# Windowed attention and a feed-forward layer: q, k, v loads, weight conversion, exponent product and order of products rewritten

## The chip, the core and the metric

The kernel runs on one core of a Trainium2 chip. A core has five engines that run their own instruction streams: TensorE (PE in the profile, its weight loads PEld), VectorE (DVE), ScalarE (ACT), GpSimd (POOL) and SyncE (SP), which here issues loads and stores. The metric is the time of one execution on the device in microseconds, the median of several runs. Before the change it is 1030.34 us.

## The reference

Eight batches of 576 positions, eight heads of 64. Attention looks back over a window of 128 positions with a linear bias per head; its output, 4608 rows of 512, goes through two matrix products with a squared, clipped activation between them.

```python
scores = scale * np.matmul(q, k.transpose(0, 1, 3, 2))
bias = slopes[:, None, None] * (-np.abs(rel).astype(np.float32))[None, :, :]
mask = (rel >= 0) & (rel < window)                      # window = 128
scores = np.where(mask, scores + bias[None], -1000000000.0)
scores = scores - np.max(scores, axis=-1, keepdims=True)
attn = np.exp(scores)
attn = attn / (np.sum(attn, axis=-1, keepdims=True) + 1e-09)
x = np.matmul(attn, v)                                  # then transposed to 4608 x 512
...
h = x @ w_in                                            # 512 x 2048
g = np.where(pos, h, np.where(neg, 0.0, (h + beta) ** 2 / (4.0 * beta)))
return (g @ w_out).astype(np.float32)                   # 2048 x 512
```

q, k and v are float32. The two weight matrices arrive as float64.

## The kernel before

The 4608 rows are cut into twelve chunks of 384 rows (NCHUNK). For each chunk there is attention for four pairs of heads (pair p, chunk p // 4, so 48 pairs) and then sixteen blocks of 128 feed-forward columns (fc). While the feed-forward of chunk c runs, the attention of chunk c + 1 is computed between its products. `segments` is the list of attention steps and `ffn` the list of feed-forward steps; the last loop (L772 to L780) writes them down interleaved, in proportion, with the attention some steps ahead. The order in which each engine then runs its instructions is made from this by a planner that simulates the program with its own costs: an instruction written down earlier has precedence, but one that is ready may go ahead of one that is not. Within one engine the order so found is fixed in the program. `behind(instructions, f)` (L241) adds that what f writes down is issued after the named instructions, as far as it runs on the same engine as they do.

Most products are made of float16 halves: a float32 value becomes a high and a low float16, and a product becomes three (high by high, high by low, low by high). In chunks 0 and 1 attention itself is in float32; from chunk 2 on (LIGHT = 2) it uses halves as well. The halves need scales, powers of two from the largest exponent of what is to be split.

A feed-forward block is `layer1` (L582: twelve products of 384 columns on PE, L585 to L587; then u on ACT, L592, g on DVE, L593 and L594, its high half on ACT, L601, its low half on POOL, L602), and two blocks later `layer2` (L605: nine products of 512 columns, L616 to L618; in chunk 0 three float32 products, L613).

The turn of a pair p from pair 8 (p8) on, as L664 to L682 write it: row maxima of pair p + 4 (`reach_of`, L308: ACT over q and k, L318, DVE over v, L384), scores of blocks 0 and 1, scores of block 2 (`scores_of_pair`, L443, PE L453; each followed by DVE L476 and ACT L478 of the softmax), the split of v (L419), the values of pair p - 1 (`values_of_pair`, L544, PE L557, then ACT L566 and DVE L567, which make the x that layer1 reads), the transposes of head 2p (`weights_t`, L492: PE L497, ACT L509, DVE L510, POOL L512 and L514), the split of q and k of pair p + 1 (L360: ACT L367, DVE L368) with the load of pair p + 5 (`load_all`, L294: q L304, k L305, v L376, all issued by SP), and the transposes of head 2p + 1. The last pair of a chunk also makes the next chunk's scales: `level` (L320) and `scale_all` (L338).

q and k of a pair of chunk 3 or later are loaded into one of five tiles, chosen by p % 5 under the names of tiles that held weights before (L301). The three-row table `rels` of biases has the sixth of those places (L354). v has six buffers.

During chunk 0 the weights are converted. The float64 numbers are loaded as pairs of 32-bit words, low and high, w_in and w_out of a block into a tile each (`fetch_weights`, L184, issued by ACT). `float32_of` (L169) scales the high word as a float on ACT (L176), brings the low word's three top bits down on ACT (L177), shifts the high word by three on DVE (L178) and adds (L179). For a scale, the row maxima of a block are spread by POOL into a diagonal matrix (`spread`, L149, L152; L335 in `level`), which PE multiplies by ones in float32 (L157, L341), so that each partition holds all maxima; DVE takes the largest and keeps its exponent bits.

Of the kernel before, what the change touches and what calls it, by code (L numbers as in the profile page):

```python
# [8 lines left out]
F32 = mybir.dt.float32  # L9
# [11 lines left out]
def windowed_attention_then_ffn(  # L21
# [94 lines left out]

    sums = const.tile([P, 2, NQB, 2], F32, name="sums")
# [17 lines left out]
    ones = const.tile([P, P], F32, name="ones")  # L135
    G.memset(ones, 1.0)
# [12 lines left out]
    def spread(name, rows):  # L149

        diag[name] = ap1.tile([P, P], F32, name=f"d_{name}", tag="d", bufs=2)
        G.tensor_scalar(diag[name], ident, rows, None, ALU.mult)  # L152

    def scale_of(name, s, i):

        b = bank(f"m_{name}")[:, :P]
        T.matmul(b, ones, diag.pop(name), start=True, stop=True)  # L157
# [11 lines left out]
    def float32_of(w, name, out=None):  # L169

        low, high = w[..., 0], w[..., 1]
        f = stg.tile([P] + list(w.shape[1:-1]), F32, name=f"f_{name}", tag="stg")
        fi = f.bitcast(I32)


        S.activation(high.bitcast(F32), high.bitcast(F32), AF.Prelu, scale=2.0 ** -112, alpha=2.0 ** 32)  # L176
        S.activation(low, low.bitcast(U32), AF.Copy, scale=2.0 ** -29)  # L177
        V.tensor_scalar(fi, high, 3, None, ALU.logical_shift_left)  # L178
        V.tensor_tensor(fi if out is None else out.bitcast(I32), fi, low, ALU.add)  # L179
        return f  # L180

    raw = {}

    def fetch_weights(fc):  # L184
        w1 = rawp.tile([P, NCC, P, 2], I32, name=f"rawi{fc}", tag=f"rawi{fc % 3}")
        S.dma_start(w1, wi32[:, 2 * fc * P:2 * (fc + 1) * P].rearrange("(c p) (f w) -> p c f w", p=P, w=2))

        w2 = rawp.tile([P, DM, 2], I32, name=f"rawo{fc}", tag=f"rawo{fc % 3}")
        S.dma_start(w2, wo32[fc * P:(fc + 1) * P, :].rearrange("p (f w) -> p f w", w=2))
        raw[fc] = (w1, w2)  # L190
# [3 lines left out]
    def convert_in(fc):  # L194
        f = wide[fc] = wp.tile([P, NCC, P], F32, name=f"f_i{fc}", tag="f_i", bufs=3)
        float32_of(raw[fc][0], f"i{fc}", out=f)
        rows = column(f"rows_i{fc}", "rows")
        V.tensor_reduce(rows, f.rearrange("p c f -> p (c f)"), X, ALU.max, apply_absolute_value=True)
        spread(f"i{fc}", rows)
# [8 lines left out]
    def split_in(fc):  # L208
        if fc > 1:
            fall_in(fc)  # L210
        f, s1 = wide.pop(fc), s_in[:, fc:fc + 1]
        t = wi[fc] = wp.tile([P, 2, NCC, P], F16, name=f"wi{fc}", tag=f"wi{fc}")
        S.activation(t[:, 0], f, AF.Copy, scale=s1)
        V.scalar_tensor_tensor(t[:, 1], f, s1, t[:, 0], ALU.mult, ALU.subtract)  # L214
# [4 lines left out]
    def convert_out(fc):  # L219
        wf[fc] = wp.tile([P, DM], F32, name=f"wf{fc}", tag=f"wf{fc}")  # L220
        float32_of(raw[fc][1], f"o{fc}", out=wf[fc])
        S.activation(junk, wf[fc], AF.Abs, accum_out=rows_o[:, fc:fc + 1])
# [70 lines left out]

    def load_all(p):  # L294
# [3 lines left out]
        if c == LIGHT:  # L298
            t = wp.tile([P, 2 * CH + P], F32, name=f"qk_{p}", tag=f"wo{NPAIR + g}")
        else:  # L300
            tag = ("rawi0", "rawi1", "rawi2", "rawo0", "rawo1")[p % 5]  # L301
            t = rawp.tile([P, 2 * CH + P], F32, name=f"qk_{p}", tag=tag)
# [17 lines left out]
    def level(c):  # L320
# [12 lines left out]
        d = diag[c] = ap1.tile([P, 2, P], F32, name=f"d_{c}", tag="qr")  # L333
        for a in range(2):
            G.tensor_scalar(d[:, a], ident, top[:, a:a + 1], None, ALU.mult)  # L335
        tops[c, "i"] = iq

    def scale_all(c):  # L338

        b = bank(f"m_{c}")[:, :2 * P]  # L340
        T.matmul(b, ones, diag.pop(c).rearrange("p a w -> p (a w)"), start=True, stop=True)  # L341
# [11 lines left out]
        if "t" not in rels:  # L353
            rels["t"] = rawp.tile([P, NQB, 2 * P], F32, name="rels", tag="rawo2")  # L354
        rels[c] = rels["t"][:, c % 2], rels["t"][:, 2]
# [279 lines left out]
    for m in range(M1):  # L635
# [11 lines left out]
        if odd:  # L647
            part["v"] = [[lambda p=p: load_v(p + 4)]] if p < NPAIR else []
            part["v"] += [[lambda x=x: load_all(x)] for x in {5: (8, 9), 6: (10,), 7: (11,)}.get(p, ())]
# [14 lines left out]
    for p in range(M1 // 2, NP):  # L664
        c, g = divmod(p, NPAIR)
        new = p + NPAIR < NP
        if new:
            segments.append([lambda p=p: reach_of(p + NPAIR)])
        segments.append([lambda p=p: scores_of_pair(p, (0, 1))])
# [141 lines left out]
```

## Time and profile before

| | |
|---|---|
| median of 3 runs | 1030.34 us (1026.98 to 1031.44) |
| profiled execution, whole | 1030.51 us |
| its span, first to last instruction | 1028.3 us |
| PE busy | 975.1 us, 95% of the span |
| DVE busy | 742.2 us, 72% |
| ACT busy | 618.2 us, 60% |
| POOL busy | 374.7 us, 36% |
| mean granted TensorE clock | 0.979 |

Busy times of an engine are times in which an instruction of it is in work; PE's products overlap, so a full PE is not yet PE at its peak. Where an engine sat idle, a row shows in brackets how long and what ended it. "x12" counts instructions. "128x384" is partitions by elements. "granted clock" is the share of TensorE's clock that the chip let through. A row that ends "busy, mean ns | idle" gives the busy time of a group, the mean of one, and the idle time of the engine just before them.

### The profile page before, as it was taken

Reading aid. Unit: us, or ns where it says so; the run is one execution under the profiler, and the core shown is the slowest. Engines: PE = TensorE matmul, PEld = TensorE weight load, DVE = VectorE, ACT = ScalarE, POOL = GpSimd, SP = SyncE. Lnnn points to the kernel's source line nnn. Section 1 sums busy time; section 2 is a strip of 40 time slices with the busy share of each in tenths; the row PEclk is TensorE's granted clock in tenths of the full one; section 3 lists DMA queues with packets and bytes.
Section 4 is the critical chain, followed back from the end, with each engine's and each line's share of the span. In section 5 each row is a group of like instructions: output and inputs, shape, how many; then the busy total and the mean of one; then the engine's idle time right before and its main releaser. Section 6 shows DMA issues by size and latency. Waiting matters only on the chain.

```text
span 1028.3 us, 17951 instructions
## 1 busy us (share of the span) xinstructions
PE 975.1 (95%) x6218; PEld 548.8 (53%) x6218; DVE 742.2 (72%) x2128; ACT 618.2 (60%) x1547; POOL 374.7 (36%) x479
## 2 busy tenths in 40 slices
PE   7579999997899899899999999999999999999998
PEld 7446554554455455455555555555555555555554
DVE  5789889887767677777777777777777867775322
ACT  4678878665756655655755765765755755654332
POOL 5332211334344323433433433433434434334221
PEclk9889999999799999999999999999999999999999
DMA  8445442002101101201211201111101100000000
GB/s 258 159 154 168 160 142 85 1 11 73 52 22 57 57 24 35 69 30 39 68 40 40 74 24 47 57 30 57 60 29 57 50 2 1 32 1 1 32 1 31
DMA packets 53275, 59.88 MB, mean 58 GB/s; under 512 B 3520, under 2 KB 42432, under 8 KB 53184
## 3 DMA queue, kind: packets, MB, share of 16 engines
q1 hardware_dynamic: 42432, 41.96, 13.0%
q10 hardware_dynamic: 10752, 16.78, 4.8%
q8 instruction: 49, 0.80, 0.3%
q14 instruction: 42, 0.34, 0.1%
HBM read 49.28 MB, written 9.44 MB: 57 GB/s over the span
## 4 chain that ended last, share of the span: by engine, by line
PE 81%; DVE 8%; DMA 4%; ACT 3%; issue 2%; POOL 1%; ACTq 0%; SPq 0%; DVEq 0%; POOLq 0%
PE h L585 11%; PE h L587 11%; PE h L586 11%; PE acc L616 11%; PE acc L617 11%; PE acc L618 11%; PE s L453 5%; PE x L557 4%; PE p L497 3%; DMA vn<-in_v_dram 2%; PE acc L613 2%; PE x L536 1%; DVE g L593 1%; ACT z L478 1%; DVE g L594 1%
## 5 line engine op out<-in xcount | busy, mean ns | idle before, releaser
L602 POOL TENSOR_TENSOR gl<-g,gh 128x384 f16<-128x384 f32 x176 | 164.8, 936 | 394.1 <-ACT gh L601 375.9
L593 DVE SCALAR_TENSOR_TENSOR g<-u,half 128x384 f32<-128x384 f32 x176 | 121.0, 689 | 178.1 <-ACT u L592 167.9
L616 PE MATMUL acc<-wo,gh 128*128 128x512 f16 x528 | 200.0, 380 | 0.4 <-ACT wo L238 0.4
L617 PE MATMUL acc<-wo,gh 128*128 128x512 f16 x528 | 200.3, 379 | 0.0
L618 PE MATMUL acc<-wo,gl 128*128 128x512 f16 x528 | 197.0, 379 | 0.0
L601 ACT CAST gh<-g 128x384 f16<-128x384 f32 x176 | 89.7, 509 | 177.3 <-DVE g L594 124.7
L592 ACT ACTIVATE u<-h,shift,fall 128x384 f32<-128x384 f32 x176 | 116.4, 664 | 88.9 <-PE h L587 88.2
L478 ACT ACTIVATE z<-z,nmax 128x256 f32<-128x256 f32 (+2 forms) x288 | 137.7, 479 | 35.5 <-DVE nmax L476 34.8
L585 PE MATMUL h<-xh,wi 128*128 128x384 f16 x448 | 146.4, 328 | 3.7 <-DVE g L594 3.7
L587 PE MATMUL h<-xh,wi 128*128 128x384 f16 x448 | 147.4, 329 | 1.3 <-DVE wi L214 1.3
L586 PE MATMUL h<-xl,wi 128*128 128x384 f16 x448 | 147.2, 328 | 0.0
L476 DVE CUSTOM_DVE_ANT_0 z<-s,rels,z_of 128x256 f32<-128x256 f32 (+2 forms) x240 | 98.4, 459 | 26.8 <-PE s L453 26.4
L594 DVE SCALAR_TENSOR_TENSOR g<-h,gain,g 128x384 f32<-128x384 f32 x176 | 107.8, 614 | 3.8
L585 PE MATMUL h<-x,wi 128*128 128x384 f16 x320 | 105.3, 331 | 4.4 <-ACT x L566 3.1
L586 PEld LDWEIGHTS <-wi 128*128 128x128 f16 x768 | 75.7, 99 | 62.2 <-issue 9.2
L585 PEld LDWEIGHTS <-wi 128*128 128x128 f16 x768 | 75.5, 98 | 62.1 <-issue 6.6
L586 PE MATMUL h<-x,wi 128*128 128x384 f16 x320 | 105.9, 331 | 0.2 <-DVE x L567 0.2
L587 PE MATMUL h<-x,wi 128*128 128x384 f16 x320 | 105.9, 331 | 0.0
L587 PEld LDWEIGHTS <-wi 128*128 128x128 f16 x768 | 75.7, 99 | 54.6 <-issue 4.2
L512 POOL TENSOR_SCALAR_AFFINE_SELECT lu<-lu 128x768 f16<-128x768 f16 x80 | 72.5, 914 | 71.0 <-DVE lu L510 56.7
L618 PEld LDWEIGHTS <-gl 128*128 128x128 f16 x528 | 51.5, 98 | 58.6 <-issue 1.1
L616 PEld LDWEIGHTS <-gh 128*128 128x128 f16 x528 | 51.6, 98 | 52.0 <-issue 2.2
(154 smaller groups left out, 1555.4 us busy)
## 6 DMA issues: line engine op xcount, KB each, us to landing
out_dram<-o SPq DMA_DIRECT2D x36, 256.0 KB, 2.1
rawi<-in_moe_w_in_dram ACTq DMA_DIRECT2D x16, 512.0 KB, 3.7
rawo<-in_moe_w_out_dram ACTq DMA_DIRECT2D x16, 512.0 KB, 4.7
vn<-in_v_dram SPq DMA_DIRECT2D x32, 256.0 KB, 3.0
qk<-in_q_dram SPq DMA_DIRECT2D x40, 192.0 KB, 3.0
qk<-in_k_dram SPq DMA_DIRECT2D x28, 256.0 KB, 3.5
vn<-in_v_dram SPq DMA_DIRECT2D x16, 192.0 KB, 2.7
qk<-in_k_dram SPq DMA_DIRECT2D x12, 192.0 KB, 2.8
```

Source lines behind the costliest of these rows:

```text
L476: V.tensor_tensor_reduce(out=z[:, i, c0:], in0=pt[:, n, c0:], in1=r[:, c0:], op0=ALU.add, op1=ALU.min, scale=factor, scalar=3.0e38, accum_ ...
L478: S.activation(z[:, i, c0:], z[:, i, c0:], AF.Exp, bias=nmax[:, i:i + 1], scale=-1.0, accum_out=sm[:, i, 0:1])
L585: T.matmul(ph, wi[fc][:, 0, cc, :], xh, start=(cc == 0), stop=False)
L586: T.matmul(ph, wi[fc][:, 0, cc, :], xl, start=False, stop=False)
L587: T.matmul(ph, wi[fc][:, 1, cc, :], xh, start=False, stop=(cc == NCC - 1))
L592: first = S.activation(u, ph, AF.Relu, bias=shift[c] if c else quarter, scale=fall[c][:, col])
L593: V.scalar_tensor_tensor(g, u, half[c] if c else 0.5, u, ALU.min, ALU.mult)
L594: last = V.scalar_tensor_tensor(g, ph, gain[c][:, col] if c else fall[c][:, col], g, ALU.mult, ALU.max)
L602: G.tensor_tensor(gl, g, gh, ALU.subtract)
L616: T.matmul(a, gh[:, ts], wo[fc][:, 0], start=first, stop=False)
L617: T.matmul(a, gh[:, ts], wo[fc][:, 1], start=False, stop=False)
L618: T.matmul(a, gl[:, ts], wo[fc][:, 0], start=False, stop=last)
```

## The change

- `load_all`: from chunk 3 on, q and k go into three tiles of two halves each that are made once and kept; a half is chosen by the pair (p // 2 % 3 and p % 2). `rels` gets a lasting tile `near` of its own, with one row for the chunk's table instead of two.
- Order of a turn from pair 8 on: load of p + 5 first, row maxima of p + 4, then the values of p - 1 and the scores of blocks 0 and 1 in one step, scores of block 2, split of v, split of q and k of p + 1, then the transposes of both heads in one step. The mark after which the next chunk's feed-forward is written down moves with the values. The loads of chunks 1 and 2 get `behind` a head's transposes.
- Weights: w_in and w_out of a block come into one tile; the two ACT instructions each take both; a shift and an or in one DVE instruction join the words. The low word's factor becomes 0.9375 of what it was.
- Exponent product: no diagonal is built. The column of maxima, read as its upper 16 bits (a bfloat16), is broadcast as the weights of a bfloat16 product with a bfloat16 identity.

```diff
-    ones = const.tile([P, P], F32, name="ones")
-    G.memset(ones, 1.0)
+    ident16 = const.tile([P, P], BF16, name="ident16")
+    G.tensor_copy(ident16, ident)
...
     def spread(name, rows):
-        diag[name] = ap1.tile([P, P], F32, name=f"d_{name}", tag="d", bufs=2)
-        G.tensor_scalar(diag[name], ident, rows, None, ALU.mult)
+        diag[name] = rows
+    def across(b, rows):
+        r = rows.bitcast(BF16)
+        for a in range(rows.shape[1]):
+            T.matmul(b[:, a * P:(a + 1) * P], r[:, 2 * a + 1:2 * a + 2].broadcast_to([P, P]), ident16, start=True, stop=True)
...
-        T.matmul(b, ones, diag.pop(name), start=True, stop=True)
+        across(b, diag.pop(name))
...
+    def fetch_weights(fc):
+        w = raw[fc] = rawp.tile([P, 2, DM, 2], I32, name=f"raw{fc}", tag=f"raw{fc % 3}")
+        S.dma_start(w[:, 0].rearrange("p (c f) w -> p c f w", c=NCC),
+                    wi32[:, 2 * fc * P:2 * (fc + 1) * P].rearrange("(c p) (f w) -> p c f w", p=P, w=2))
+        S.dma_start(w[:, 1], wo32[fc * P:(fc + 1) * P, :].rearrange("p (f w) -> p f w", w=2))
+    def unfold(fc, which=slice(0, 2)):
+        low, high = raw[fc][:, which, :, 0], raw[fc][:, which, :, 1]
         S.activation(high.bitcast(F32), high.bitcast(F32), AF.Prelu, scale=2.0 ** -112, alpha=2.0 ** 32)
-        S.activation(low, low.bitcast(U32), AF.Copy, scale=2.0 ** -29)
-        V.tensor_scalar(fi, high, 3, None, ALU.logical_shift_left)
-        V.tensor_tensor(fi if out is None else out.bitcast(I32), fi, low, ALU.add)
+        S.activation(low, low.bitcast(U32), AF.Copy, scale=0.9375 * 2.0 ** -29)
+    def float32_of(fc, a, out):
+        V.scalar_tensor_tensor(out.bitcast(I32), raw[fc][:, a, :, 1], 3, raw[fc][:, a, :, 0], ALU.logical_shift_left, ALU.bitwise_or)
...
     def load_all(p):
-            tag = ("rawi0", "rawi1", "rawi2", "rawo0", "rawo1")[p % 5]
-            t = rawp.tile([P, 2 * CH + P], F32, name=f"qk_{p}", tag=tag)
+            i = p // 2 % 3
+            if i not in two:
+                two[i] = rawp.tile([P, 2, 2 * CH + P], F32, name=f"qk_{p}", tag=f"raw{i}")
+            t = two[i][:, p % 2]
...
-        if "t" not in rels:
-            rels["t"] = rawp.tile([P, NQB, 2 * P], F32, name="rels", tag="rawo2")
-        rels[c] = rels["t"][:, c % 2], rels["t"][:, 2]
+        rels[c] = near[:, 0], near[:, 1]
...
-            part["v"] = [[lambda p=p: load_v(p + 4)]] if p < NPAIR else []
-            part["v"] += [[lambda x=x: load_all(x)] for x in {5: (8, 9), 6: (10,), 7: (11,)}.get(p, ())]
+            part["v"] = [[lambda p=p: behind(done_t[2 * p], lambda: load_v(p + 4))]] if p < NPAIR else []
+            part["v"] += [[lambda p=p, x=x: behind(done_t[2 * p - 1], lambda: load_all(x))] for x in {5: (8, 9), 6: (10,), 7: (11,)}.get(p, ())]
...
-    for p in range(M1 // 2, NP):
+    for p in range(p8, NP):
         c, g = divmod(p, NPAIR)
         new = p + NPAIR < NP
-        if new:
+        if p + 5 < NP:
+            segments.append([lambda p=p: load_all(p + 5)])
+        if new and p > p8:
             segments.append([lambda p=p: reach_of(p + NPAIR)])
-        segments.append([lambda p=p: scores_of_pair(p, (0, 1))])
+        segments.append(([lambda p=p: values_of_pair(p - 1)] if p > p8 else []) + [lambda p=p: scores_of_pair(p, (0, 1))])
+        if p > p8 and g == 0:
+            ready.append(len(segments))
         if new and g == NPAIR - 1:
             segments.append([lambda c=c: level(c + 1)])
         segments.append([lambda p=p: scores_of_pair(p, (2,))])
         segments.append([lambda p=p: split_v(p)])
-        if p > M1 // 2:
-            segments.append([lambda p=p: values_of_pair(p - 1)])
-            if g == 0:
-                ready.append(len(segments))
+        if p == p8:
+            segments.append([lambda p=p: reach_of(p + NPAIR)])
         if new and g == NPAIR - 1:
             segments.append([lambda c=c: scale_all(c + 1)])
-        segments.append([lambda p=p: weights_t(2 * p)])
-        segments.append(([lambda p=p: split_qk(p + 1)] if p + 1 < NP else []) + ([lambda p=p: load_all(p + 5)] if p + 5 < NP else []))
-        segments.append([lambda p=p: weights_t(2 * p + 1)])
+        if p + 1 < NP:
+            segments.append([lambda p=p: split_qk(p + 1)])
+        segments.append([lambda p=p: weights_t(2 * p), lambda p=p: weights_t(2 * p + 1)])
```

More of the change, by code (lines that the diff above doesn't have):

```diff
@@ L115, in windowed_attention_then_ffn @@
                     compare_op=ALU.is_ge, fill=NEG)
+    near = const.tile([P, 2, 2 * P], F32, name="near")
     sums = const.tile([P, 2, NQB, 2], F32, name="sums")
@@ L167, in windowed_attention_then_ffn @@
     wo32 = w_out.bitcast(I32)
[L169 to L176, printed above, removed]
-        S.activation(low, low.bitcast(U32), AF.Copy, scale=2.0 ** -29)
-        V.tensor_scalar(fi, high, 3, None, ALU.logical_shift_left)
-        V.tensor_tensor(fi if out is None else out.bitcast(I32), fi, low, ALU.add)
-        return f
     raw = {}
     def fetch_weights(fc):
[L185 to L190, printed above, removed]
+        w = raw[fc] = rawp.tile([P, 2, DM, 2], I32, name=f"raw{fc}", tag=f"raw{fc % 3}")
[4 more added lines that the diff above has]
+        low, high = raw[fc][:, which, :, 0], raw[fc][:, which, :, 1]
+        S.activation(high.bitcast(F32), high.bitcast(F32), AF.Prelu, scale=2.0 ** -112, alpha=2.0 ** 32)
+        S.activation(low, low.bitcast(U32), AF.Copy, scale=0.9375 * 2.0 ** -29)
+    def float32_of(fc, a, out):
+        V.scalar_tensor_tensor(out.bitcast(I32), raw[fc][:, a, :, 1], 3, raw[fc][:, a, :, 0], ALU.logical_shift_left, ALU.bitwise_or)
     wide = {}
     def convert_in(fc):
-        f = wide[fc] = wp.tile([P, NCC, P], F32, name=f"f_i{fc}", tag="f_i", bufs=3)
-        float32_of(raw[fc][0], f"i{fc}", out=f)
+        f = wide[fc] = wp.tile([P, DM], F32, name=f"f_i{fc}", tag="f_i", bufs=3)
+        unfold(fc)
+        float32_of(fc, 0, f)
         rows = column(f"rows_i{fc}", "rows")
-        V.tensor_reduce(rows, f.rearrange("p c f -> p (c f)"), X, ALU.max, apply_absolute_value=True)
+        V.tensor_reduce(rows, f, X, ALU.max, apply_absolute_value=True)
         spread(f"i{fc}", rows)
@@ L211, in split_in @@
         f, s1 = wide.pop(fc), s_in[:, fc:fc + 1]
-        t = wi[fc] = wp.tile([P, 2, NCC, P], F16, name=f"wi{fc}", tag=f"wi{fc}")
+        t = wp.tile([P, 2, DM], F16, name=f"wi{fc}", tag=f"wi{fc}")
+        wi[fc] = t.rearrange("p s (c f) -> p s c f", c=NCC)
         S.activation(t[:, 0], f, AF.Copy, scale=s1)
@@ L220, in convert_out @@
         wf[fc] = wp.tile([P, DM], F32, name=f"wf{fc}", tag=f"wf{fc}")
-        float32_of(raw[fc][1], f"o{fc}", out=wf[fc])
+        float32_of(fc, 1, wf[fc])
         S.activation(junk, wf[fc], AF.Abs, accum_out=rows_o[:, fc:fc + 1])
@@ L292, in load_qk @@
             DMA.dma_start(kr[r, j, :n], k[g * P + j * D:g * P + (j + 1) * D, (c + 1) * CH - n:(c + 1) * CH])
+    two = {}
     def load_all(p):
@@ L332, in level @@
         V.tensor_reduce(top[:, 1:2], tops.pop(c)[:, :NPAIR], X, ALU.max)
-        d = diag[c] = ap1.tile([P, 2, P], F32, name=f"d_{c}", tag="qr")
-        for a in range(2):
-            G.tensor_scalar(d[:, a], ident, top[:, a:a + 1], None, ALU.mult)
+        diag[c] = top
         tops[c, "i"] = iq
@@ L340, in scale_all @@
         b = bank(f"m_{c}")[:, :2 * P]
-        T.matmul(b, ones, diag.pop(c).rearrange("p a w -> p (a w)"), start=True, stop=True)
+        across(b, diag.pop(c))
         i_2[c], s_2[c] = column(f"i_2{c}", "i_2", 3, 2), column(f"s_2{c}", "s_2", 3, 2)
```

## The prediction

> **What bounds the kernel now.** I read the page first, then the busy time by stretches cut at each chunk's first L594 (16 of that line in each stretch, one chunk of the feed-forward), then the timeline where a stretch is long.
>
> ```profile
> span 1028.3 us, 17951 instructions
> ...
> PE 975.1 (95%) x6218; PEld 548.8 (53%) x6218; DVE 742.2 (72%) x2128; ACT 618.2 (60%) x1547; POOL 374.7 (36%) x479
> ```
> ```profile
> 66.20:174.00 107.80, 100.71 (x447) 58.65 (x448) 97.22 (x305) 90.52 (x208) 23.86 (x36) 0.98 0.45 149
> 174.00:267.80 93.80, 82.14 (x543) 45.29 (x543) 77.33 (x208) 60.56 (x151) 32.80 (x34) 0.93 0.12 38
> 267.80:347.90 80.10, 77.16 (x506) 41.96 (x506) 58.15 (x169) 47.73 (x124) 31.48 (x38) 0.98 0.13 41
> 347.90:430.10 82.20, 78.15 (x530) 42.91 (x530) 58.10 (x169) 48.04 (x124) 31.56 (x40) 0.98 0.14 45
> ...
> 506.70:583.60 76.90, 76.90 (x514) 42.22 (x512) 58.02 (x166) 46.84 (x123) 30.28 (x38) 1.00 0.15 48
> 583.60:659.80 76.20, 76.20 (x531) 42.25 (x529) 58.19 (x166) 47.75 (x123) 30.93 (x40) 1.00 0.14 43
> ```
>
> The columns after the length are PE, PEld, DVE, ACT and POOL busy, then granted clock and DMA. From 430 us on a chunk takes 76.2 to 76.9 us and PE has no idle time: there only less PE work, or fewer changes between its shapes, can gain. Three chunks are longer than that mean of 76.55: by 17.25 (93.80), 3.55 (80.10) and 5.65 us (82.20), 26.45 together. The chunk in which the weights are converted takes 107.80 with DVE at 97.22, PE at 100.71 and ACT at 90.52: three engines near full, so neither alone is the limit. With the 26 us ahead of it:
>
> ```profile
> sum 134.00, PE 118.91 PEld 72.15 DVE 118.80 ACT 109.20 POOL 33.36; mean PE 19.82 PEld 12.03 DVE 19.80 ACT 18.20 POOL 5.56
> ```
>
> From 40 to 174 us PE is idle for 134.00 - 118.91 = 15.1 us.
>
> The 17.25 us lie at one place, on PE, then on the other engines:
>
> ```profile
> 248.87 1.15 PE L497 MATMUL p<-ident,ep 128*128 128x128 f32 x6
> 251.88 0.23 PE L453 MATMUL s<-h 64*128 64x128 f16 x2 [1.86 <-ACT h L367]
> ...
> 257.63 0.79 PE L453 MATMUL s<-h 64*128 64x256 f16 x5 [3.38 <-DVE nmax L476]
> 258.35 2.13 PE L557 MATMUL x<-lu,vs 128*64 128x256 f16 x24
> 263.55 0.80 PE L585 MATMUL h<-x,wi 128*128 128x384 f16 x2 [3.07 <-ACT x L566]
> ...
> 268.57 0.48 PE L585 MATMUL h<-x,wi 128*128 128x384 f16 x1 [1.34 <-DVE g L594]
> ```
> ```profile
> 254.38 1.06 POOL L514 TENSOR_SCALAR_AFFINE_SELECT lu<-lu 128x768 f16<-128x768 f16 x1
> ```
> ```profile
> 253.61 0.34 SPq L304 DMA_DIRECT2D qk<-in_q_dram  x1
> ```
> ```profile
> 256.79 0.52 ACT L318 ACTIVATE junk<-qk 128x384 bf16<-128x384 f32 x1 [4.46 <-DMA qk<-in_q_dram]
> ...
> 263.03 0.47 ACT L566 ACTIVATE x<-x 128x384 f16<-128x384 f32 x1
> ```
>
> The feed-forward of chunk 2 (L585) needs x of pair 11, the result of the values product L557. That product's weights were ready when POOL ended, 254.38 + 1.06 = 255.4, but it stood on PE behind the scores of pair 12 (251.88, 257.63) and ran at 258.35. Its copy L566 then stood on ACT behind softmax work that had been held 4.46 us by L318, a row maximum of q that waited for a load issued at 253.61 only. So two causes are in series: the order values after scores, and late loads.
>
> **The change part by part.**
>
> *Loads a turn ahead, six halves.* `load_all(p+5)` goes from the end of turn p to its start, and the slot it writes was last read by pair p-1 (six halves), not by p (five tags). Its three triggers cost SP 0.34 us each or a little more and SP is idle most of the time; behind them stand only later loads and the stores. The wait that this can shorten is
>
> ```profile
> ACT junk L318 <- DMA qk<-in_q_dram: 43.1, 23, 4.5
> ```
>
> 43.1 us of ACT's idle time; on PE it shows only where PE has nothing else queued, which is the 26.45 us above. But L318 runs as soon as the written-out order thinks its load has landed, and pair 18's load still follows the split of pair 12 in the same way; so I do not count the ACT wait as gone. The `behind` around the early loads ties instructions of one engine; the loads are issued by SP, the named instructions by ACT, DVE and POOL, so I cost it at nothing. Were it to hold the loads back, it could lose no more than the 15.1 us over again.
>
> *Values ahead of scores.* In the new order the values of p-1 come first, then the scores (0, 1) of p. At the place above the product could start at 255.4 instead of 258.35, its copy would be ahead of pair 12's softmax on ACT, and L585 could go on at about 255.4 + 1.2 (24 products at full clock) + 0.5 (L566) + 0.5 (DVE's low half, taken as long as ACT's) = 257.6 instead of 263.55: 5.9 us. With L585 running, the 1.34 us at 268.57 has cover, and of the 17 us at half clock around it (granted clock 0.93 over the stretch, 0.07 x 93.8 = 6.6 us of PE's time) I take 3. So 10 of the 17.25 us, bounds 0 and 17.25. The same two causes stand at 330 and 425 us; of 3.55 + 5.65 = 9.2 I take 4, bounds 0 and 9.2.
>
> *In the steady chunks* the groups of one turn are
>
> ```profile
> 599.07 0.82 PE L497 MATMUL p<-ident,ep 128*128 128x128 f32 x6
> ...
> 599.82 0.28 PE L453 MATMUL s<-h 64*128 64x256 f16 x1
> ...
> 604.52 0.82 PE L453 MATMUL s<-h 64*128 64x256 f16 x12
> ...
> 604.85 1.67 POOL L514 TENSOR_SCALAR_AFFINE_SELECT lu<-lu 128x768 f16<-128x768 f16 x2
> ...
> 609.92 0.42 PE L453 MATMUL s<-h 64*128 64x192 f16 x5
> ...
> 610.27 1.18 PE L557 MATMUL x<-lu,vs 128*64 128x256 f16 x24
> ```
>
> one score alone, eleven and one, then five and 24 values. After the change 24 values and twelve scores stand together and six scores by themselves: the number of groups between feed-forward products stays, except that the lone score may vanish or another appear. A lone one costs at most its 0.28 us; over 32 turns of eight chunks 9 us either way. I take 0.
>
> *Shift-or and joined tile.* Per block DVE now runs two pairs of
>
> ```profile
> L179 DVE CUSTOM_DVE_ANT_0 wf<-rawo,f_o 128x1024 uint16<-128x1024 uint16 x16 | 11.5, 720 | 0.0
> ...
> L593 DVE SCALAR_TENSOR_TENSOR g<-u 128x384 f32<-128x384 f32 x16 | 9.1, 572 | 3.1 <-ACT u L592 2.9
> ...
> L176 ACT ACTIVATE rawi<-rawi 128x512 f32<-128x512 f32 x16 | 10.8, 678 | 4.8 <-DMA kz<-in_k_dram 2.8 <-issue 1.2 <-ACT lu L501 0.6
> ...
> L178 DVE TENSOR_SCALAR f_i<-rawi 128x512 int32<-128x512 int32 x16 | 6.8, 423 | 0.3 <-ACT rawi L176 0.3
> ```
>
> L178 and L179, 0.42 + 0.72 = 1.14 us. One scalar_tensor_tensor of 512 elements takes their place. Its nearest row is L593 with constants, 0.572 us for 384; the step from 384 to 512 is
>
> ```profile
> L368 DVE SCALAR_TENSOR_TENSOR h<-qk,s_k,h 128x512 f16<-128x512 f32 x2 | 1.4, 738 | 0.0
> L368 DVE SCALAR_TENSOR_TENSOR h<-qk,s_q,h 128x384 f16<-128x384 f32 x2 | 1.2, 613 | 0.1
> ```
>
> 0.125 us, so 0.70 us: 0.44 less, 32 times, 14 us of DVE. ACT's four instructions of 0.67 become two of 1024 elements. The step by size on ACT:
>
> ```profile
> 24.48 0.39 ACT L478 ACTIVATE z<-z,nmax 128x128 f32<-128x128 f32 x1
> ...
> 24.86 0.49 ACT L478 ACTIVATE z<-z,nmax 128x256 f32<-128x256 f32 x1
> ```
>
> 0.10 per 128, so 0.67 + 0.40 = 1.07 each: 2.68 becomes 2.14, 16 x 0.54 = 8.6 us of ACT. Against it w_in's float32 waits for both, 2.14 instead of 1.34 us, and the first of them for the second landing too; the loads run two blocks (2 x 6.7 us) ahead, which covers that, and L592 can stand up to 0.4 us longer behind an ACT instruction.
>
> *Bfloat16 product of exponents.* The diagonal that POOL built goes; PE takes the column itself.
>
> ```profile
> PE m_i L157 <- POOL d_i L152: 6.8, 5, 3.2
> ...
> PE m_x L157 <- POOL d_x L152: 3.4, 2, 2.1
> ```
> ```profile
> L152 POOL TENSOR_SCALAR d_i<-ident,rows_i x16: 599/802/1965, 35.0 to 155.1; 128x128 f32<-128x128 f32 x16
> ```
>
> Seven waits of PE, 10.2 us; with 0.8 us less ahead of each, about 5.6 go. Together with DVE's 14 and ACT's 8.6 this acts on the 15.1 us that PE idles from 40 to 174; PE's own 118.9 us stay. I take half, 7 us; bounds 0 and 15.1. From chunk 2 on the two float32 products of a chunk go:
>
> ```profile
> 246.69 0.59 PE L341 MATMUL m<-d,ones 128*128 128x256 f32 x2
> 247.12 0.38 PE L618 MATMUL acc<-wo,gl 128*128 128x512 f16 x1
> ```
>
> 0.43 us from one start to the next. Two bfloat16 ones of 128 columns are not in the trace; below they cost nothing, above as much as two of the six float32 transposes at 599.07 (0.75 / 6 = 0.125 each). I take the upper one, 0.43 - 0.25 = 0.18, ten times: 2 us, bounds 2 and 4. The single `near` tile for the mask makes L356 wait for the last L476 of the chunk before, on the same engine and in that order already: nothing.
>
> **The sum.** 10 + 4 + 0 + 7 + 2 = 23 us less. The profiled execution took 1030.5 us (span 1028.3 and 2.2 around it), the median of the runs 1030.3, so no correction: 1007.5 us.
>
> [...]
>
> **Rivals.**
>
> *Half rate of shift-or.* If the two bitwise steps cost twice the streaming, 0.20 + 2 x 0.50 = 1.20 us against 1.14: DVE gains nothing and the half of 15.1 falls to the POOL part alone, about 2. Then 1030.5 - 18 = 1012.5. The float32 rows speak against it. Chance 0.05.
>
> *The loads and the order were not what held.* At 251.88 PE waited for the split of pair 12, whose scale needs all four pairs; at 248.87 for the softmax. If these follow the new order as they did the old one, and the conversion stretch is held by PE, only 2 or 3 us are left: 1028. For it speaks that L318 can again be issued before its load has landed; against it that L557 was ready 3 us before it ran. Chance 0.15.
>
> *A new wait: values for POOL (slower).* After the transposes at 599.07 the last POOL select ends at 604.85 + 1.67 = 606.5, but the scores went at 604.52 and the values only at 610.27, 3.8 us after POOL. If the values stand where the scores stood, PE waits up to 606.5 - 604.5 = 2.0 us in each of 40 turns. Above 23 / 40 = 0.6 us a turn the change loses. At 1 us: 1007.5 + 40 = 1047. Against it: the written order comes from a planner that knows POOL's work, and feed-forward products can stand in between. Chance 0.15.
>
> *All of it.* 17.25 + 9.2 + 15.1 + 4 = 45.5 us less, 985. Chance 0.15.
>
> **How the numbers follow.** My forecast has 0.50, with its own range of 995 to 1020. Less than 0.5%, about 5 us, cannot be told from no change: faster holds the forecast, the half rate and all of it, 0.70; same 0.15; slower 0.15. The range goes to 982 (all of it, and a few of the 9 us of lone scores) and to 1042 (most of the new wait).
>
> **What would show it.** Right: no PE idle time over 2 us between 245 and 270, clock 1.00 there, L557 ahead of the next pair's first L453; the three long chunks nearer to 76.5; the conversion chunk near 101, one DVE row near 0.70 us in place of two. Wrong: PE waiting at L557 for POOL turn after turn, the chunks from 430 us on longer than 77, or DVE's shift-or at 1.2 us. If the chunks from 430 on change by over 1 us each, my zero for the grouping was the mistake.

## The result and the profile after

The changed kernel takes 1142.44 us (median of 4 runs, the kernel before 1030.12 beside it): 1.108 times as long, 95% interval 1.104 to 1.113. The forecast was 1007.5 us, so even its sign was wrong. One of the four, the one first profiled, took 1364.22 us at a mean granted clock of 0.73, with 0.75 for up to 232 us on end; it is left out of the ratio, and the rows below are those of the next profiled run (1138.5 us, mean granted clock 0.939).

Span, busy time of the engines, and the granted clock in 40 slices, after:

```profile
span 1136.8 us, 17773 instructions
...
PE 1009.0 (89%) x6199; PEld 560.2 (49%) x6199; DVE 739.1 (65%) x2096; ACT 626.8 (55%) x1515; POOL 341.5 (30%) x440
...
PEclk9899999988998998997998999899799899799899
```

The span grew by 108.5 us. DVE, ACT and POOL have about as much work as before, or less. PE's busy time grew by 33.9 us with 19 instructions fewer, and its idle time from 53.2 to 127.8 us, by 74.6. So two thirds of the loss is idle time of PE. The other third is nearly the same products at a lower clock: the mean granted clock fell from 0.979 to 0.939, and the stretches at half clock grew from 46 to 142 us. The 24 products of the values took 2.13 us at a granted clock of 0.50 and 1.18 us at 1.00 (258.35 and 610.27 in the prediction); so half of PE's busy time in these stretches, an estimate of what the lower clock cost, is 12 us before and 45 after. From the tenth slice on the clock dips every three or four slices; a slice is 28.4 us, so that is about once a chunk.

The same stretches as in the prediction, cut at each chunk's first second half of g (now L598), after:

```profile
66.20:166.00 99.80, 93.40 (x417) 54.41 (x418) 90.71 (x282) 87.17 (x181) 10.71 (x18) 1.00 0.48 160
166.00:263.20 97.20, 83.32 (x548) 44.74 (x546) 75.59 (x208) 61.86 (x150) 29.88 (x32) 0.91 0.13 42
263.20:349.60 86.40, 78.33 (x506) 42.48 (x507) 56.80 (x165) 48.84 (x124) 28.80 (x34) 0.95 0.14 42
349.60:441.60 92.00, 81.21 (x530) 43.90 (x530) 59.98 (x169) 48.65 (x123) 30.45 (x38) 0.95 0.12 36
...
534.70:622.20 87.50, 80.12 (x506) 43.19 (x507) 56.04 (x164) 48.70 (x124) 28.88 (x34) 0.93 0.13 41
622.20:714.50 92.30, 81.41 (x530) 43.97 (x530) 60.99 (x168) 48.67 (x122) 30.21 (x38) 0.94 0.12 36
```

The conversion chunk is 8.0 us shorter (107.80 to 99.80). Every chunk behind it is longer, by 116.5 us together, and the steady ones now take 85 to 94 us: that is where the time went. Before they took 73.9 to 77.0; the 76.2 to 76.9 of the prediction are two of these seven chunks. Three waits on PE stand out; of them only the first is among the waits listed for the kernel before, with 5.0 us:

```profile
PE h L589 <- DVE g L598: 31.4, 8, 5.9
PE x L561 <- POOL lu L518: 30.5, 14, 6.3
PE p L501 <- DVE ep L493: 17.1, 5, 5.0
```

One turn of a steady chunk on PE (start, length, line, output<-inputs, shapes, count; the products of the feed-forward, L589 to L591 and L620 to L622, are left out):

```profile
559.97 0.82 PE L501 MATMUL p<-ident,ep 128*128 128x128 f32 x6
...
568.29 0.30 PE L561 MATMUL x<-lu,vs 128*64 128x256 f16 x1
568.52 0.28 PE L457 MATMUL s<-h 64*128 64x128 f16 x4
568.74 1.01 PE L561 MATMUL x<-lu,vs 128*64 128x256 f16 x17
569.68 0.56 PE L457 MATMUL s<-h 64*128 64x128 f16 x8
...
574.16 0.28 PE L457 MATMUL s<-h 64*128 64x256 f16 x1
575.13 0.50 PE L457 MATMUL s<-h 64*128 64x256 f16 x5
...
582.06 0.82 PE L501 MATMUL p<-ident,ep 128*128 128x128 f32 x6
...
591.03 0.30 PE L561 MATMUL x<-lu,vs 128*64 128x256 f16 x1
591.25 0.29 PE L457 MATMUL s<-h 64*128 64x128 f16 x4
```

And what the values (L561) of 591.03 stand for, on POOL:

```profile
584.26 0.86 POOL L516 TENSOR_SCALAR_AFFINE_SELECT lu<-lu 128x768 f16<-128x768 f16 x1 [2.35 <-DVE lu L514]
...
585.95 0.86 POOL L516 TENSOR_SCALAR_AFFINE_SELECT lu<-lu 128x768 f16<-128x768 f16 x1
586.77 1.99 POOL L518 TENSOR_SCALAR_AFFINE_SELECT lu<-lu 128x768 f16<-128x768 f16 x2
```

Read the turn as a chain. Transposes at 582.06; copies on ACT and DVE; POOL's four selects, done at 586.77 + 1.99 = 588.8; values at 591.03; and only among the values, from 591.3 on, the next pair's scores, whose softmax must pass before their transposes can come. In the rows of the kernel before that the prediction shows, the scores of the next pair (604.52) stood ahead of the values (610.27), so that POOL's work of one pair (604.85 to 606.5) and the softmax of the next ran at the same time. Its first DVE step, before:

```profile
605.38 0.48 DVE L476 CUSTOM_DVE_ANT_0 z<-s,rels,z_of 128x256 f32<-128x256 f32 x1 [0.55 <-PE s L453]
```

Now one pair's attention follows the other's end to end: 591.03 - 568.29 = 22.7 us. Four of them are 91 us, and the steady chunks take 85 to 94.

The same for 32 turns (pairs 12 to 43), worked out from the starts of these products on PE, means in us; the twelfth score is the last of blocks 0 and 1:

| kernel | 12th score to last transpose | last transpose to next pair's 12th score | last transpose to first values | turn |
|---|---|---|---|---|
| before | 13.60 | 5.79 | 11.06 | 19.38 |
| after | 14.67 | 7.92 | 6.26 | 22.59 |

3.21 us a turn, 32 times, is 103 of the 116.5 us. The values come 4.8 us earlier than before, as was meant; the scores, which start the next pair's chain, come 2.1 us later, and their way to the last transpose takes 1.1 us more.

While a turn lasts PE has feed-forward products to run. At a chunk's end they run out, because the next chunk's need the values of the last pair. PE there, after:

```profile
605.72 0.82 PE L501 MATMUL p<-ident,ep 128*128 128x128 f32 x6
...
610.45 0.27 PE L561 MATMUL x<-lu,vs 128*64 128x256 f16 x1 [0.30 <-POOL lu L518]
...
612.23 0.98 PE L561 MATMUL x<-lu,vs 128*64 128x256 f16 x17 [0.74 <-POOL lu L518]
...
614.64 0.24 PE L457 MATMUL s<-h 64*128 64x192 f16 x1 [1.43 <-DVE nmax L480]
...
622.91 0.48 PE L589 MATMUL h<-x,wi 128*128 128x384 f16 x1 [4.80 <-DVE g L598]
```

PE waits for the select, for the softmax, and then 4.80 us for the first g of the new chunk, with nothing else to run. Around this gap 0.50 of the clock was granted, from 614.8 to 628.4 us, and the steady chunks have a granted clock of 0.92 to 0.95 where they had 0.98 to 1.00.

What the change did to the conversion chunk can be read from the groups of 40 to 174 us before and 40 to 166 us after, on PE (busy us, mean ns | idle us ahead of the group, and what ended it). Before:

```profile
L157 PE MATMUL m_i<-d_i,ones 128*128 128x128 f32 x30 | 6.6, 300 | 7.0 <-POOL d_i L152 6.8
...
L157 PE MATMUL m_x<-d_x,ones 128*128 128x128 f32 x4 | 1.0, 326 | 3.4 <-POOL d_x L152 3.4
```

After:

```profile
L501 PE MATMUL p<-ident,ep 128*128 128x128 f32 x33 | 5.5, 276 | 4.3 <-ACT xh L582 2.4 <-DVE ep L493 1.9
...
L159 PE MATMUL m_i<-ident,rows_i 128*128 128x128 bf16 x15 | 3.3, 220 | 0.8 <-DVE rows_i L201 0.8
...
L159 PE MATMUL m_x<-ident,rows 128*128 128x128 bf16 x2 | 0.4, 219 | 0.0
```
```profile
40.00:166.00 126.00, 112.15 (x523) 68.78 (x523) 111.74 (x358) 107.92 (x232) 16.41 (x32) 0.99 0.50 162
```

The 10.2 us of waits for POOL's diagonal are gone, but PE still idles 126.00 - 112.15 = 13.9 us, against 15.1: other waits (4.3 us ahead of the transposes, 0.3 before) took their place. Of the 8.0 us, 6.8 came out of PE's busy time, 118.91 to 112.15. The m_i and m_x rows give 7.6 - 3.7 = 3.9 of that: the 15 and 2 float32 products ran as 30 and 4 instructions, the bfloat16 ones as 15 and 2. Much of the rest came with the clock: 0.97 was granted over 40 to 174 us before, with 0.83 from 60 to 80, and 0.99 over 40 to 166 after.

DVE and ACT in the conversion, groups by shape over the whole span, after:

```profile
L187 ACT ACTIVATE raw<-raw 128x1024 f32<-128x1024 f32 x16 | 18.4, 1151 | 4.8 <-DMA kz<-in_k_dram 3.7 <-ACT lu L505 0.6 <-issue 0.4
...
L192 DVE SCALAR_TENSOR_TENSOR wf<-raw 128x512 int32<-128x512 int32 x16 | 12.2, 762 | 0.0
...
L192 DVE SCALAR_TENSOR_TENSOR f_i<-raw 128x512 int32<-128x512 int32 x16 | 11.0, 688 | 1.0 <-ACT raw L188 0.7
```

### The profile page after: what moved, and what is told of

The parts are those of the page before. It is cut to its first block, busy times and chain, and to the rows that moved or that the text cites. A ratio compares the mean times of both kernels' runs of the same rounds, so it can differ in the third digit from the quotient of the medians.

```text
span 1362.5 us, 17773 instructions
## 1 busy us (share of the span) xinstructions
PE 1260.8 (93%) x6199; PEld 633.3 (46%) x6199; DVE 738.7 (54%) x2096; ACT 633.8 (47%) x1515; POOL 336.0 (25%) x440
## 4 chain that ended last, share of the span: by engine, by line
PE 84%; DVE 7%; DMA 4%; ACT 3%; issue 1%; POOL 1%; SPq 0%; ACTq 0%; DVEq 0%
PE h L589 12%; PE h L590 12%; PE h L591 12%; PE acc L620 11%; PE acc L621 11%; PE acc L622 11%; PE s L457 4%; PE acc L617 4%; PE x L561 3%; DMA vn<-in_v_dram 3%; PE p L501 3%; ACT z L482 1%; PE x L540 1%; DVE g L597 1%; DMA raw<-in_moe_w_out_dram 1%
## 5 line engine op out<-in xcount | busy, mean ns | idle before, releaser
L597 DVE SCALAR_TENSOR_TENSOR g<-u,half 128x384 f32<-128x384 f32 x176 | 113.0, 642 | 362.1 <-ACT u L596 336.1
L620 PE MATMUL acc<-wo,gh 128*128 128x512 f16 x528 | 244.3, 463 | 0.0
L621 PE MATMUL acc<-wo,gh 128*128 128x512 f16 x528 | 243.1, 460 | 0.0
L622 PE MATMUL acc<-wo,gl 128*128 128x512 f16 x528 | 237.5, 462 | 0.0
L589 PE MATMUL h<-xh,wi 128*128 128x384 f16 x448 | 176.4, 396 | 18.3 <-DVE g L598 17.1
L591 PE MATMUL h<-xh,wi 128*128 128x384 f16 x448 | 178.3, 398 | 0.0
L590 PE MATMUL h<-xl,wi 128*128 128x384 f16 x448 | 178.0, 397 | 0.3 <-DVE xl L583 0.2
L480 DVE CUSTOM_DVE_ANT_0 z<-s,near,z_of 128x256 f32<-128x256 f32 (+2 forms) x240 | 99.0, 460 | 87.2 <-PE s L457 87.1
L590 PEld LDWEIGHTS <-wi 128*128 128x128 f16 x768 | 87.7, 114 | 120.5 <-issue 68.5
L589 PE MATMUL h<-x,wi 128*128 128x384 f16 x320 | 126.7, 399 | 16.9 <-DVE g L598 15.2
L589 PEld LDWEIGHTS <-wi 128*128 128x128 f16 x768 | 87.3, 114 | 92.6 <-issue 40.3
L591 PE MATMUL h<-x,wi 128*128 128x384 f16 x320 | 128.4, 401 | 0.0
L590 PE MATMUL h<-x,wi 128*128 128x384 f16 x320 | 128.0, 400 | 0.2
L591 PEld LDWEIGHTS <-wi 128*128 128x128 f16 x768 | 88.7, 116 | 80.9 <-issue 13.5
L598 DVE SCALAR_TENSOR_TENSOR g<-h,gain,g 128x384 f32<-128x384 f32 x176 | 108.1, 615 | 3.9
L622 PEld LDWEIGHTS <-gl 128*128 128x128 f16 x528 | 58.4, 111 | 83.2 <-issue 75.6
L561 PE MATMUL x<-lu,vs 128*64 128x256 f16 (+1 forms) x888 | 70.6, 296 | 24.6 <-POOL lu L518 24.6
```

Source lines behind the costliest of these rows:

```text
L561: T.matmul(px[r, q0 * P:q1 * P], vs[:, a, i + b0, r], lus[j][:, b, first:first + q1 - q0, :].rearrange("p a w -> p (a w)"), start=(n == 0) ...
L589: T.matmul(ph, wi[fc][:, 0, cc, :], xh, start=(cc == 0), stop=False)
L590: T.matmul(ph, wi[fc][:, 0, cc, :], xl, start=False, stop=False)
L591: T.matmul(ph, wi[fc][:, 1, cc, :], xh, start=False, stop=(cc == NCC - 1))
L597: V.scalar_tensor_tensor(g, u, half[c] if c else 0.5, u, ALU.min, ALU.mult)
L598: last = V.scalar_tensor_tensor(g, ph, gain[c][:, col] if c else fall[c][:, col], g, ALU.mult, ALU.max)
```

## Experiments

The causes that were to be told apart: the order of values and scores; the new place of the loads; that values and scores stand in one step; the lead with which the attention is written down; POOL's selects; and the parts that have nothing to do with the order (halves, joined tile, shift-or, product). Each comparison is with the kernel before on the same chip, 1029.5 to 1031.0 us. Chunk lengths are cut as above.

**The changed kernel again.** No edit.

> The changed kernel once more, for a profile at full granted clock. Its earlier profile, at a granted clock of about 0.75, shows at each chunk boundary the first products of the next chunk (L589) held some 6 us for DVE's L598. Theory A (order): values of p-1 and scores of p in one step make the turn one serial chain (scores, softmax, transposes, POOL, values, next scores), so x of the last pair comes after the chunk's feed-forward products have run out; expects the idle time again at 9 or 10 boundaries, 5 to 8 us each, with half clock behind each, 1135 to 1145 us. Theory B (loads): DVE and ACT are held by row maxima of v, q, k whose loads come late; expects the same time, but DVE and ACT idle for DMA inside each boundary for most of the PE idle time.

1138.61 us, ratio 1.104 (1.096 to 1.112). The slowdown is there again; its trace is the one read above.

**The old turn.** The turn loop of the kernel before (values behind the split of v, transposes apart, loads after the split), all else changed; then the same with the load at the turn's start; then the changed loop with only the values and the ready mark moved back.

```diff
 # old turn
-        if p + 5 < NP:
-            segments.append([lambda p=p: load_all(p + 5)])
-        segments.append(([lambda p=p: values_of_pair(p - 1)] if p > p8 else []) + [lambda p=p: scores_of_pair(p, (0, 1))])
+        segments.append([lambda p=p: scores_of_pair(p, (0, 1))])
...
+            segments.append([lambda p=p: values_of_pair(p - 1)])
...
+        segments.append(([lambda p=p: split_qk(p + 1)] if p + 1 < NP else []) + ([lambda p=p: load_all(p + 5)] if p + 5 < NP else []))
```

> The changed kernel with the turn order of the kernel before (loop from pair 8 on, loads at the end of a turn); halves, joined weight tile, shift-or and bfloat16 product stay. Theory A: the loss goes, 1005 to 1030 us. Theory B with the loss in the halves: still above 1090 us.

> As the kernel with the old turn order, but the load of pair p + 5 at the start of turn p as in the change. Theory A: within 8 us of the run with loads at the end of a turn. Theory B with the loss in the early loads (v's load in front of others in SP's queue): 1090 us or more, and ACT's wait for q above 40 us in total.

> The changed kernel with one thing undone: the values of p - 1 (and the mark for the next chunk) go back behind the split of v, everything else of the new turn order stays. Theory A, with the values ahead of the scores as the cause: 1005 to 1040 us. If instead the two transposes in one step, or the split of q and k ahead of them, is the cause: still above 1090 us.

Old turn 1038.18 us (1.008, 1.005 to 1.011); with the early load 1031.97 (1.0025, 1.0002 to 1.0048); values alone moved back 1038.38 (1.008, 1.006 to 1.010). Moving the values back undoes 100 of the 109 us with the early loads, the joined transposes and all the rest in place. The place of the loads is worth 6 us, in favour of the early one. The table's numbers for the old turn are 13.57, 6.23, 11.57 and 19.80.

None of the three is faster than before, though each keeps the gain of the conversion chunk (99.7 to 100.4 us). That is the second question below.

**The order alone.** In the kernel before, only the values and the ready mark are moved ahead of the scores, into one step with them; and in the changed kernel only the two halves of that step are swapped.

```diff
 # values first, in the kernel before
-        segments.append([lambda p=p: scores_of_pair(p, (0, 1))])
+        segments.append(([lambda p=p: values_of_pair(p - 1)] if p > M1 // 2 else []) + [lambda p=p: scores_of_pair(p, (0, 1))])
...
 # swapped, in the changed kernel
-        segments.append(([lambda p=p: values_of_pair(p - 1)] if p > p8 else []) + [lambda p=p: scores_of_pair(p, (0, 1))])
+        segments.append([lambda p=p: scores_of_pair(p, (0, 1))] + ([lambda p=p: values_of_pair(p - 1)] if p > p8 else []))
```

> The kernel before with one part of the change alone: the values of p - 1 in one step ahead of the scores of blocks 0 and 1 of p, with the mark for the next chunk behind them. Theory A (serial turn): the chain scores, softmax, transposes, POOL selects, values, next scores takes some 23 us a turn, 92 a chunk, so 1110 to 1145 us without any other part of the change. Rival: the values ahead of the scores cost that much only together with the early loads or the other parts; then under 1060 us.

> The changed kernel with the two calls inside the one step exchanged: scores of p first, then values of p - 1. Theory A: the scores no longer stand behind POOL's selects, 1010 to 1050 us. Rival (one step of 36 products, with its changes of shape, is what costs): still above 1100 us.

Values first in the kernel before: 1134.89 us (1.102, 1.097 to 1.106), 104 us and so nearly the whole loss by one edit. Scores first within the step in the changed kernel: 1037.96 (1.0075, 1.003 to 1.012). It is not the joined step, nor the ready mark, which stays in place in the swapped kernel, but which of the two stands first. The turns:

| kernel | 12th score to last transpose | last transpose to next pair's 12th score | last transpose to first values | turn |
|---|---|---|---|---|
| before, values first | 14.68 | 7.64 | 6.03 | 22.32 |
| after, scores first | 14.00 | 5.89 | 7.09 | 19.89 |

The waits of PE in the kernel before with values first are those of the changed kernel (L557 and L514 are the changed kernel's L561 and L518):

```profile
PE p L497 <- DVE ep L489: 24.9, 6, 5.0
PE h L585 <- DVE g L594: 20.8, 6, 5.1
PE x L557 <- POOL lu L514: 20.6, 12, 5.6
```

**The lead.** If the attention only came too late, writing it down four steps earlier should help.

```diff
-            emit_attention(int(now + (end - now) * (r + (4 if c else 7)) / STEPS))
+            emit_attention(int(now + (end - now) * (r + (8 if c else 7)) / STEPS))
```

> The changed kernel with attention written down 8 steps of 32 ahead of the feed-forward instead of 4. Theory A: a turn still takes some 23 us, so a chunk still 92; 1115 us or more (a later start is bought once, not per chunk). Rival (the mark moved, so x comes one step late at each boundary): the boundary waits go, under 1060 us.

1137.42 us (1.104, 1.097 to 1.112), the same turn of 22.59 us. Here the chain is longer than its cover, and an earlier start doesn't help.

**POOL's second select.** Without it the weights stay unmasked on the causal side, so the output is another one; done in the changed kernel and in the kernel before.

```diff
-        gg = G.affine_select(out=flat[:, 1::2, :], in_=flat[:, 1::2, :], pattern=[[0, 2 * NQB], [1, P]],
-                             base=0, channel_multiplier=-1, compare_op=ALU.is_ge, fill=0.0)
-        done_t[m] = [ga.ins, gv.ins, gg.ins]
+        done_t[m] = [ga.ins, gv.ins]
```

> The changed kernel without the second of POOL's two selects per head (the causal side of the weights is left unmasked, so the output is another). Two selects of 0.85 us less in each turn's chain. Theory A: a turn is 1.7 us shorter, four per chunk and nine chunks bound by it, about 60 us less: 1070 to 1095 us. Rival (POOL is not in the chain that sets the turn): within 10 us of the changed kernel.

> The kernel before without the second of POOL's selects per head (the causal side of the weights is left unmasked, so the output is another). In the changed kernel the same edit brought 35 us. Theory A: in the old order POOL's selects are not in the chain that sets the turn, so within 8 us of the kernel before. Rival (POOL's time counts in either order): 990 to 1005 us.

Changed kernel 1103.66 us (1.071, 1.067 to 1.076), 35 less than with the select. Kernel before 1028.41 (one run), nothing. The same 1.7 us of POOL a pair are free where the next pair's scores overlap them and on the path where they don't: the turn is 21.66 us, 0.93 less, 32 times 30 us. The select is a third of the loss and not, as the expectation had it, about half: the values then come 4.73 us behind the transposes instead of 6.26, and the rest of the chain stays.

**Shift-or and product, one by one,** on the kernel before, and the changed tiles and conversion without the product, old turn.

```diff
 # shift-or
-        V.tensor_scalar(fi, high, 3, None, ALU.logical_shift_left)
-        V.tensor_tensor(fi if out is None else out.bitcast(I32), fi, low, ALU.add)
+        V.scalar_tensor_tensor(fi if out is None else out.bitcast(I32), high, 3, low, ALU.logical_shift_left, ALU.bitwise_or)
...
 # product
-        T.matmul(b, ones, diag.pop(name), start=True, stop=True)
+        across(b, diag.pop(name))
```

> The kernel before with shift-or alone. If the shorter conversion itself moves the later order: chunks 4 to 8 at 78 to 81 us, 1028 to 1036 us. If the product of exponents does that: chunks 4 to 8 at 76 to 77 us and 1018 to 1026 us.

> The kernel before with the bfloat16 product of exponents alone. If the product moves the later order: chunks 4 to 8 at 78 to 81 us and 1030 to 1040 us; if the shift-or does, they stay at 76 to 77 us and the total is 1020 to 1030 us.

> The kernel before with two parts of the change alone: shift-or in one DVE instruction (weights of a block still in two tiles) and the bfloat16 product of exponents. In the runs of the changed kernel the conversion chunk took 99.8 instead of 107.8 us with either order. Theory: these two parts bring it, and the later chunks stay at 76 to 77 us: 1016 to 1024 us. Rival: the 8 us are lost again after that chunk whatever is changed (the attention behind it is the limit): 1026 to 1032 us.

> The kernel before with shift-or and the bfloat16 product, and attention written down 8 steps of 32 ahead instead of 4. Theory: in the old order the turns overlap, and what is late at the ends of chunks 1 to 3 (17, 4 and 6 us) is bought back by an earlier start: 1000 to 1015 us. Rival: those waits come from scales that need all four pairs and do not move: within 5 us of the run with 4 steps.

> The changed kernel with the old turn order and with the old product of exponents (POOL's diagonal, float32): halves, lasting bias tile, joined weight tile and shift-or stay. With the new product and the old order chunks 4 to 8 took 78 to 80 us instead of 76 to 77. If the halves or the bias tile cost that: again 78 to 80 in these chunks, 1032 to 1042 us. If the product costs it: 76 to 77, 1018 to 1028 us.

The last two columns are of the profiled execution of each.

| kernel | us | ratio (95%) | end of the conversion chunk | fifth to ninth chunk, mean |
|---|---|---|---|---|
| before | 1030.1 | 1 | 174.1 | 76.5 |
| shift-or alone | 1017.0 | 0.988 (0.983 to 0.993) | 173.4 | 76.5 |
| product alone | 1040.5 | 1.011 (1.004 to 1.017) | 173.9 | 80.4 |
| both | 1033.6 | 1.004 (1.003 to 1.006) | 168.1 | 79.4 |
| both, lead 8 | 1030.7 | 1.001 (0.9995 to 1.003) | 171.2 | 79.6 |
| halves, joined tile, shift-or | 1047.4 | 1.017 (1.015 to 1.020) | 174.7 | 80.2 |
| all, old turn | 1038.2 | 1.008 (1.005 to 1.011) | 166.0 | 79.0 |

Neither edit alone ends the conversion earlier by more than 0.7 us; both together by 6 (with lead 8 by 3), all by 8: in that chunk ACT, DVE and PE were all near full (90.52, 97.22 and 100.71 of 107.80 us), and a gain on one engine showed only with the others. The 13 us that shift-or alone gains lie elsewhere: 11.6 of them in the chunk behind the conversion, 82.20 us for 93.80. And each kernel that has the product or the halves loses 2.5 to 3.9 us a chunk in the mean of the fifth to ninth, where the edit itself does next to nothing (two products a chunk; another address for the same data). There the old turn's kernel shows, on PE, at a chunk's end:

```profile
579.93 0.32 PE L589 MATMUL h<-x,wi 128*128 128x384 f16 x1 [3.16 <-DVE g L598]
```

and on ACT, then on DVE, ahead of the g it waited for:

```profile
575.09 0.52 ACT L326 ACTIVATE junk<-qk 128x384 bf16<-128x384 f32 x1 [1.47 <-DMA qk<-in_q_dram]
...
576.26 1.24 ACT L625 ACTIVATE o<-acc,o_g 128x512 f32<-128x512 f32 x2
...
577.40 1.23 ACT L596 ACTIVATE u<-h,shift,fall 128x384 f32<-128x384 f32 x2
```
```profile
577.43 0.55 DVE L388 TENSOR_REDUCE rows<-vn 128x1 f32<-128x384 f32 x1 [1.48 <-DMA vn<-in_v_dram]
```

The row maxima of the pair four ahead (L326, L388) stand in ACT's and DVE's fixed order ahead of the output copy and of u and g, before their loads have landed. Each wait is 1.5 us here. The one on ACT held the output copy, then u, then the g that PE stood for; the one on DVE cost nothing at this place, because L388 had ended at 578.0, before u was there (578.1). The kernel before has such waits too (45.5 us on ACT for q and k, 56.1 in the old turn's kernel), but its PE has hardly any idle time in these chunks, so they fell where PE had other products.

**Row maxima tied to the transposes.** If that is the cause, the row maxima may only be issued later. They are put behind the last instructions of the transposes of the pair before, in four kernels: both edits on the kernel before; all with old turn and early load; shift-or alone; and the changed kernel with its order as it is.

```diff
-            segments.append([lambda p=p: reach_of(p + NPAIR)])
+            segments.append([lambda p=p: behind(done_t[2 * p - 1], lambda: reach_of(p + NPAIR))])
```

> Shift-or and product in the old order, and the row maxima of pair p + 4 issued on ACT and DVE behind the transposes' copies of the turn before. If the 2 to 3 us at each chunk end are ACT and DVE standing at row maxima for loads just issued: the waits of L318's line for DMA fall below 15 us in total and the total comes to 1005 to 1020 us. If not: within 5 us of 1033.5.

> The changed kernel in the old turn order with early loads (1032.0 us), and the same tie of the row maxima. If the row maxima's waits are the cause: 1005 to 1022 us; if not, within 5 us of 1032.

> The kernel before with shift-or alone and the tied row maxima, without the new product. If the tie works by itself as in the two tied runs (999.2 and 1001.1 us): 996 to 1008 us, and the product is worth no more than a few us. If it needs the product: above 1010 us.

> The changed kernel as it is, with the row maxima tied behind the transposes' copies of the turn before. Theory A (serial turn): the turn still takes 22 to 23 us, above 1100 us. Rival (the late loads make up most of the 100 us): under 1060 us.

| kernel | us without | us with the tie | ratio to before (95%) |
|---|---|---|---|
| shift-or and product | 1033.6 | 999.2 | 0.971 (0.966 to 0.975) |
| all, old turn, early load | 1032.0 | 1001.1 | 0.972 (0.967 to 0.978) |
| shift-or | 1017.0 | 1004.2 | 0.975 (0.971 to 0.979) |
| the changed kernel | 1138.6 | 1100.9 | 1.069 (1.064 to 1.075) |

The tie is worth 13 to 38 us. With it the waits of ACT's row maxima for loads fall to 0.3 us or less in all four kernels; that it gains by ending these waits, and not by another order that came with the tie, is the likely reading, which no run separates. Shift-or alone with the tie ends the conversion chunk at 168.1 us instead of 173.4, so there too such waits may have hidden a gain. Without the tie the product costs 17 us on top of shift-or (1017.0 to 1033.6); with the tie that loss is gone, and it may be a gain of 5 (1004.2 to 999.2, though the two intervals overlap). The fastest, page and its sixth chunk:

```profile
span 997.5 us, 17795 instructions
...
PE 964.0 (97%) x6199; PEld 542.0 (54%) x6199; DVE 743.6 (75%) x2096; ACT 614.0 (62%) x1547; POOL 342.6 (34%) x440
...
PEclk9799999999999999999999999999999999999999
```
```profile
479.60:552.10 72.50, 72.50 (x493) 39.76 (x491) 59.51 (x167) 45.69 (x123) 29.20 (x35) 1.00 0.16 50
```

That chunk is the shortest of its fifth to ninth, which take 75.2 us in the mean, 79.4 without the tie. Of row maxima that wait for loads its waits still list one row, where the same kernel without the tie has 46.2 us on ACT for q, 6.3 for k and 18.8 on DVE for v:

```profile
DVE rows L385 <- DMA vn<-in_v_dram: 8.6, 6, 3.8
```

In the changed order the tie takes 38 us too, but 22.59 becomes only 21.59 us a turn: the chain is still the bound.

## Why the prediction was wrong

- **The failed step** is "In the steady chunks": it counted the groups of products, found their number unchanged, and took 0 (9 us either way). What the move changed was not the number of groups but what the scores come behind: 3.21 us a turn, 103 us. The row of 604.52 ahead of 610.27 was in the prediction, and what it says, that the next pair is started while POOL still masks the last one, was not read out of it. The prediction had named a sign for this, chunks from 430 us on that change by over 1 us each; they grew by 9 to 17.
- **Values ahead of scores** was to give 10 us at one chunk's end and 4 at two others. The product did come earlier behind its transposes (6.26 against 11.06 us), but these chunks became longer (93.80 to 97.20, 80.10 to 86.40, 82.20 to 92.00). The prediction followed the late values at one chunk's end and not the scores that they displace. The place itself can gain without the move: with shift-or alone in the old order the first of these chunks takes 82.20. The prediction's sentence that the step loses above 0.6 us a turn was right; the 40 turns lost 2.6 us each by the move alone (1134.9 - 1031.0, over 40).
- **The slower rival** named the mechanism's place, values that wait for POOL where the scores stood, with a price of up to 2.0 us a turn and 0.15. It priced PE's own wait. What runs out is the chain behind PE: the scores are late by the wait, the softmax by the scores, and the next values by the softmax, and around the chunk's end the granted clock was lower too (0.50 from 614.8 to 628.4 us). Its listed waits (30.5 us in 14 places) are less than a third of the loss.
- **A planner that knows POOL's work** was the argument against that rival. It did fill the turn with feed-forward products, as the prediction hoped, up to the chunk's end, and there had none left.
- **Loads.** Their place is worth 6 us. "L318 can again be issued before its load has landed" was right, and was used only as a reason why little might be gained (the rival of 1028); that these waits could get costlier with any edit was not seen. Taking them away is worth 13 to 38 us.
- **Conversion.** 7 us forecast over 40 to 174, 8 measured. That the sizes agree is in part luck: the waits for POOL went and others came in their place, so that only 1.2 us of idle time were saved, while "PE's own 118.9 us stay" missed the 3.9 us that the products of one instruction save and the higher clock (0.99 for 0.97).
- **Sizes.** Shift-or 0.70 us forecast, 0.69 and 0.76 measured; the rival's 1.20, whose 0.20 is what 0.70 leaves beyond four steps of 0.125, did not come. Why the one-source shift before took only 0.42 us for the same 512 elements (L178), no run here shows. ACT over 1024 elements 1.07 forecast, 1.15 measured. The two products of a chunk: the 20 float32 instructions of the whole span become 20 bfloat16 ones of 0.22 us, a gain of 2 to 4 us that no run separates.

**Open.** For the scores of 591.3 the split of their q and k had ended at 577.2 and the banks were copied out by 584.7; why the written order nevertheless kept them until the values were ready isn't in the trace. Nor is why the product and the halves move the waits for loads to the chunk ends. The joined tile, the halves and the `behind` around the early loads were not tried each by itself, nor was the tie on the kernel before without any other edit.

## What to carry to other kernels

When two groups of products are exchanged, don't count groups: ask which of the two starts the longest chain on other engines, and put that one first (here 1037.96 us against 1138.61). A product that ends a chain may wait behind other work, as the values did before, 11.06 us behind the transposes; one that starts a chain delays everything after it, here by 3.21 us a turn, and PE stood idle for it where the cover ran out. Where a schedule is fixed beforehand, an instruction that reads a load can be put ahead of its landing (43.1 us of ACT's waits for q before); tie it to an instruction that surely comes later, before judging small edits, because such waits can move to and from the critical place when the order changes, as they seem to have done here.

## What the runs showed of the hardware

In the profile before, the granted clock was 0.50 from 254.4 to 271.3 us and 1.00 from 583.6 to 659.8. Products of 384 columns that followed each other started 0.32 us apart in the first stretch and 0.16 in the second.

In the changed kernel 74.6 us more of idle time on PE stood beside a mean granted clock of 0.939 instead of 0.979, and beside 33.9 us more of busy time for 19 fewer instructions. With shift-or, product and tie PE idled 997.5 - 964.0 = 33.5 us, beside 0.991. Whether the one brought the other no run separates.

A bitwise shift-or of two int32 operands took 0.69 to 0.76 us on DVE for 512 elements, where the float32 rows give an estimated 0.70.
